# A mirrored table copied by another DMA queue, a mirrored column by matrix products, mirrored rows in four transfers

## The chip, the cores and the metric

The kernel runs on one core of one Trainium2 chip. The metric is the device time of one execution in microseconds (us). Profiles come from the hardware profiler, of one execution. Engines: PE is TensorE (PEld its weight loads), ACT ScalarE, DVE VectorE, POOL GpSimd, SP SyncE. Here SP issues nearly all DMAs, and POOL the few that copy from DRAM to DRAM with rows turned round; each of the two has a DMA queue of its own.

## The reference

Two independent layers over 2048 tokens of width 448, their outputs side by side:

```python
# A: Fourier mixing, real part of a 2-D DFT
a = einsum("bsd,ed->bse", x, dft_hid_re);  b = einsum("bsd,ed->bse", x, dft_hid_im)
y = einsum("ts,bse->bte", dft_seq_re, a) - einsum("ts,bse->bte", dft_seq_im, b)
# B: attention with 16 heads of 28
q, k, v = split(x @ wqkv);  p = softmax(q @ k.T * 28 ** -0.5);  o = (p @ v) @ wo
out = concatenate([y, o], axis=-1)
```

The inputs are float32, and so is the output.

## The kernel before

**Work.** Attention (B) runs head by head: scores (L1404, 128 keys by 512 queries), exp on ACT (L1408), and a pack of 32 products with the values (L1415) for every 16 scores. Scores need ACT, which is slower than PE at this, so PE fills the time between them with the other work, in this order: the projections to q, k and v (L619), the feature transform of layer A (L871, `hidden_both`), its sequence transform, real part (part 0) and imaginary part (part 1) (L1145, `sequence_halved`), and the output projection (L1646).

**Symmetry in layer A.** The DFT tables are symmetric, so the kernel multiplies with a quarter of the sequence table and reads the rest of it only to compare it with the mirrored quarter: the differences go through small products too, and a flag at the end repeats everything in a plain way (`If(again != 0)`) if a difference is above 2^-17 of the largest entry. For the comparison three things are needed in mirrored order:

- the mirrored table `turned_d` (basd in the profile): for each part 8 x 128 rows of 2 KB, read from the table with a negative row step and written to DRAM, in 9 DMAs of up to 256 KB (`turn_table`). The sequence transform loads it (L1118).
- the mirrored column: the column 0 of block row 8, 4 x 128 numbers in reverse order. `turn_table` copies it from the table to DRAM (`row_d`, rowd in the profile), with a last dimension of one element; `columns` loads it (`turn`, L1019) and subtracts it from the column itself (L1026).
- the mirrored rows of the transformed features (`turned_ab`, abt in the profile): for each of four groups one DMA of 4 x 127 rows of 1792 bytes, from `ab_d` (abd in the profile), plus a small one for the first row (`turn_rows`, L940 and L944). `combine` loads them (L957).

All three kinds of copies are issued by POOL, through `move`.

**Order.** The program's order is written out ahead of time by a planner (`Schedule.run`) in the kernel's Python code: each task has engines with assumed durations, a key (its due time in the planner's units), dependencies and slots of buffers. Each engine takes the ready task with the lowest key; a task with `hold=True` isn't taken before the work on PE has come near its key. A DMA task on SP is modelled with a size (the KB moved), an extra latency, a flow of all DMAs and at most 8 in flight; a task of `move` only with a duration on POOL and a latency, without any flow. Each engine then runs its own list in order, and a wait in it holds all that stands behind.

```python
    def dma(key, emit, size=256, extra=0.0, n=1, **kw):
        return sch.add({"SP": 0.4}, key, lambda e: emit(), dmas=[(size, extra)] * n, **kw)
    def move(key, emit, d, lat, **kw):
        return sch.add({"POOL": d}, key, lambda e: emit(), lat=lat, **kw)
    ...
    for part in range(2):
        turn_table(part, 120.0 + 200.0 * part)
    turn_rows()
```

The feature transform starts at the key `h_at` (304.8 by the planner's constants) and ends at `s_at` (474.1). Buffers that matter here: `kept`, 20 tiles of 128 x 2 x 512 floats, which hold exp's output, the loads and results of layer A and staged outputs; 8 PSUM banks.

**Start.** SP loads the inputs (xb, wqkv, xa), stores the first q and k to DRAM (L664, L665, qkd in the profile) and loads pieces of them (L1385, qb), with which PE computes a first maximum (L1388). The values' projection (L619, "wd,xt") runs around these.

Of the kernel before, what the change touches and what calls it, by code (L numbers as in the profile page):

```python
# [11 lines left out]
F32 = mybir.dt.float32  # L12
# [316 lines left out]
def tile_kernel(ctx, tc, xa, wre, wim, wd, xb, wqkv, wo, out):  # L329
# [25 lines left out]
    row_d = [dram.tile([FT, P], F32, name=f"rowd{i}") for i in range(2)]  # L355
# [4 lines left out]
    ident = new("ident", [P, P])  # L360
# [26 lines left out]
    turn = new("turn", [P, FT])  # L387
# [26 lines left out]
    make_identity(nc, ident)  # L414
    nc.gpsimd.memset(sums, 0.0)
# [434 lines left out]

    def hidden_both(ready):
        for g in PAIRS_AT:
            x, ld = rows_both(g, fkey(0, 0) - 13)
            for a in range(2):
                st = g + a * HT
                key = fkey(1, F_ROWS)
                hi, lo, h, l = folded(x, ld, a, key - 9)
                pair = kept_s.slot()
                of = lambda w, i: w.t[:ROWS[i % 2], i]
                seq = []  # L860
                for i in range(4):
                    c0, c1 = (0, EVEN) if i < 2 else (EVEN, 2 * MAIN)
                    seq += [(hi, i, lambda i=i: table(i, "main"), 0, 2 * MAIN, M448), (lo, i, lambda i=i: table(i, "hi"), c0, c1, MLOW),
                            (hi, i, lambda i=i: low_at(i), c0, c1, MLOW)]
                rest = [(hi, i, lambda i=i: table(i, "rest"), 0, 2 * REST, M448) for i in range(4)]
                at = key
                ends = []
                for b, (seq, o) in enumerate(((seq, fill_s.slot()), (rest, fill_s.slot()))):
                    for n, (w, i, y, c0, c1, d) in enumerate(seq):
                        def emit(e, w=w, i=i, y=y, c0=c0, c1=c1, o=o, n=n, m=len(seq) - 1):  # L870
                            nc.tensor.matmul(o.t[:, c0:c1], of(w, i), y(), start=n == 0, stop=n == m)  # L871
                        last[0] = pe(at, emit, d=d, deps=[last[0], *([h, *ready] if n == 0 else [l] if n == 1 else [])],
                                     use=[hi, lo, o, *low_in, *([pair] if n == len(seq) - 1 else [])])
                        at += d
                    ways = ((0, 0, EVEN), (1, EVEN, 2 * MAIN)) if b == 0 else ((None, 0, 2 * REST),)
                    for e, c0, c1 in ways:
                        to = lambda pair=pair, e=e: pair.t[:, :, MAIN:D] if e is None else pair.t[:, :, e:MAIN:2]
                        ends.append(sch.add({"ACT": 0.43 if e is None else 0.3, "DVE": 0.53 if e is None else 0.32}, key - 10,
                                            lambda w, o=o, to=to, c0=c0, c1=c1: copy_of(w, to(), halves(o.t[:, c0:c1])), deps=[last[0]], use=[o, pair]))
                ab_done[st] = dma(key - 10, lambda pair=pair, st=st: nc.sync.dma_start(ab_d[st % HT][st // HT].rearrange("b p d -> p b d"), pair.t[:, :, :D]), 448, deps=ends, use=[pair])  # L880
# [26 lines left out]
    def move(key, emit, d, lat, **kw):  # L907

        return sch.add({"POOL": d}, key, lambda e: emit(), lat=lat, **kw)

    base_turned, ab_turned, row_turned = {}, {}, {}

    def turn_table(part, key):
        src = wim if part else wre
        row, to = NT * P, turned_d[part]
        for n, p in enumerate(range(1, P, 16)):
            r = min(16, P - p)

            def put(p=p, r=r):
                nc.gpsimd.dma_start(rows_at(to, p * FT * P, [[P * FT * P, HT], [FT * P, r], [1, FT * P]]),  # L920
                                    rows_at(src, (P - p) * row, [[P * row, HT], [-row, r], [1, FT * P]]))
            base_turned[part, n] = move(key + n * 4, put, 1.5, 12.0, hold=True)

        def first():
            nc.gpsimd.dma_start(rows_at(to, 0, [[P * FT * P, HT], [1, FT * P]]), rows_at(src, P, [[P * row, HT], [1, FT * P]]))
            at = HT * P * row
            nc.gpsimd.dma_start(rows_at(row_d[part], 1, [[P, FT], [1, P - 1], [1, 1]]), rows_at(src, at + (P - 1) * row, [[P, FT], [-row, P - 1], [1, 1]]))
            nc.gpsimd.dma_start(rows_at(row_d[part], 0, [[P, FT], [1, 1]]), rows_at(src, at + P, [[P, FT], [1, 1]]))
        row_turned[part] = base_turned[part, HT] = move(key + HT * 4, first, 2.5, 12.0, hold=True)

    def turn_rows():
        none = kept_s.slot()
        z = pool(0.0, lambda: nc.gpsimd.memset(none.t[:1], 0.0), 0.6, use=[none])
        ab_turned[0, 0] = dma(0.0, lambda: nc.sync.dma_start(rows_at(turned_ab[0], 0, [[P * D, 2], [1, D]]), none.t[:1, :, :D]), 4, deps=[z], use=[none])
        ab_turned[0, 1] = dma(0.0, lambda: nc.sync.dma_start(rows_at(turned_ab[0], 2 * P * D, [[P * D, 2], [1, D]]), none.t[:1, :, :D]), 4, deps=[z], use=[none])
        for g in range(FT):
            far = HT - 1 - g

            def put(g=g, far=far):
                nc.gpsimd.dma_start(rows_at(turned_ab[g], D, [[P * D, 4], [D, P - 1], [1, D]]), rows_at(ab_d[far], (P - 1) * D, [[P * D, 4], [-D, P - 1], [1, D]]))  # L940
            ab_turned[g, 2] = move(0.0, put, 1.5, 16.0, deps=[ab_done[far], ab_done[far + HT]])
            if g:
                def first(g=g):
                    nc.gpsimd.dma_start(rows_at(turned_ab[g], 0, [[P * D, 4], [1, D]]), rows_at(ab_d[HT - g], 0, [[P * D, 4], [1, D]]))  # L944
                ab_turned[g, 0] = move(0.0, first, 1.2, 5.0, deps=[ab_done[HT - g], ab_done[NT - g]])

    def combine(part, at, after):
        half = lambda s, i, n=D: s.t[:, i, :n]
        minus, plus = (ALU.add, ALU.subtract) if part else (ALU.subtract, ALU.add)

        def group(g):
            key = at(g)
            x, y, m = kept_s.slot(), kept_s.slot(), kept_s.slot()
            ld = dma(key, hold=True, emit=lambda: nc.sync.dma_start(x.t[:, :, :D], ab_d[g][:, part].rearrange("a p d -> p a d")),
                     size=448, deps=[ab_done[g], ab_done[g + HT]], use=[x])

            lm = dma(key + 1, hold=True, emit=lambda: nc.sync.dma_start(m.t[:, :, :D], turned_ab[g][:, part].rearrange("a p d -> p a d")),  # L957
                     size=448, deps=[ab_turned[g, n] for n in range(3) if (g, n) in ab_turned], use=[m])
# [16 lines left out]
        def plain(h):  # L975
            key = at(h) + 1
            x = kept_s.slot()
            ld = dma(key, hold=True, emit=lambda: nc.sync.dma_start(x.t[:, :, :LOW], ab_d[FT + h][:, part, :, :LOW].rearrange("a p d -> p a d")),
                     size=226, deps=[ab_done[FT + h], ab_done[FT + h + HT]], use=[x])
# [32 lines left out]
    def columns(part, key, after, after_all):  # L1012
# [6 lines left out]
        lr = dma(key, lambda: nc.sync.dma_start(turn, row_d[part].rearrange("f p -> p f")), 16, extra=4.0, deps=[*after, row_turned[part]])  # L1019
        if part:  # L1020
            lr = pool(key, lambda: nc.gpsimd.memset(turn[:1, FT - 1:], 0.0), 0.1, deps=[lr])
# [3 lines left out]
        for t in (FT, HT + FT):  # L1025
            d.append(dve(key, lambda t=t: nc.vector.tensor_tensor(dmid[:, t:t + FT], raw[:, t:t + FT], back(turn, 0, FT), op=op), 0.2, deps=[ld, lr]))  # L1026
# [5 lines left out]
    def special(part, key, after):  # L1032
# [5 lines left out]
        def put():  # L1038
            nc.sync.dma_start(w.t.rearrange("p a b -> p (a b)")[:65:32], rows_at(src, FT * P, [[0, 3], [P * row, HT], [1, P]]))
            nc.sync.dma_start(x.t[:65:32, :, :D], rows_at(ab_d[FT], part * P * D, [[0, 3], [2 * P * D, 2], [1, D]]))  # L1040
            if part == 0:
                nc.sync.dma_start(x.t[:65:32, 0, D:D + 1], rows_at(src, HT * P * row + FT * P, [[0, 3], [1, 1]]))
# [5 lines left out]
        if part == 0:  # L1048
            one = lambda p0=0: x.t[p0:96, 0, D:D + 1]
# [3 lines left out]
        both = lambda i, p0=0, p1=96: x.t[p0:p1, i, :D]  # L1053
# [471 lines left out]
    for part in range(2):  # L1525
        turn_table(part, 120.0 + 200.0 * part)
# [251 lines left out]
```

## Time and profile before

| | |
|---|---|
| time, median of 3 runs | 842.19 us (836.09 to 845.36) |
| the profiled execution | 837.84 us, span 836.0 us |
| mean granted TensorE clock | 0.975 |
| PE busy | 804.3 us (96%) |
| ACT busy | 572.4 us (68%) |
| DVE busy | 441.5 us (53%) |
| POOL busy | 73.6 us (9%) |
| moved by DMA | 155.29 MB, mean 186 GB/s |

The profiled execution is one of the program's; its span runs from the first to the last instruction. "Granted clock" is the share of the full TensorE clock that was let through; a PE that is busy at a low clock does less. A row of the chain of work gives its start, its duration and what it was. Rows of an engine's timeline give start, duration, line, operation, tiles (written <- read) and how often; in brackets the idle time before it and what ended that. For DMAs issued by POOL the last number is the median time from issue to landing.

### The profile page before, as it was taken

How to read it: one execution, taken by the hardware profiler on the slowest of the kernel's cores; microseconds unless marked ns; L12 is line 12 of the kernel's file. 1: busy time of each engine (PE TensorE's matmuls, PEld its weight loads, DVE VectorE, ACT ScalarE, POOL GpSimd, SP SyncE). 2: the span in 40 equal slices, each digit the busy share in tenths (PEclk: the TensorE clock that was granted, in tenths of full speed). 3: DMA queues.
4: the chain of work that ended last, by engine and by line, in shares of the span. 5: the costliest groups of instructions: out<-in, count | busy, mean ns of one | idle time of the engine just before them, and what ended most of it. 6: DMA issues, size and time to landing. Idle time of an engine off the chain costs nothing.

```text
span 836.0 us, 14227 instructions
## 1 busy us (share of the span) xinstructions
PE 804.3 (96%) x4713; PEld 483.5 (58%) x4713; DVE 441.5 (53%) x913; ACT 572.4 (68%) x1162; POOL 73.6 (9%) x230
## 2 busy tenths in 40 slices
PE   8779999999999889999999999999999999999986
PEld 6667555575565455566554555555545555555666
DVE  6523224354153223253432877868898876794551
ACT  5202887657878646887878676777787777878922
POOL 5200000000010200000000111011111110110000
PEclk9889999999999969999999999999999999999999
DMA  7996856643354764545546887686878677764533
GB/s 246 229 193 208 267 161 204 197 165 104 118 165 111 148 107 116 169 133 183 146 130 201 208 255 239 199 264 191 261 162 276 212 217 250 236 219 147 164 124 107
DMA packets 149159, 155.29 MB, mean 186 GB/s; under 512 B 41992, under 2 KB 118374, under 8 KB 149078
## 3 DMA queue, kind: packets, MB, share of 16 engines
q1 hardware_dynamic: 143638, 146.40, 60.6%
q0 software_dynamic: 5440, 7.91, 3.2%
q8 instruction: 39, 0.64, 0.3%
q14 instruction: 42, 0.34, 0.2%
HBM read 112.78 MB, written 50.99 MB: 196 GB/s over the span
## 4 chain that ended last, share of the span: by engine, by line
PE 81%; DMA 14%; ACT 1%; DVE 1%; SPq 1%; issue 1%; DVEq 0%; ACTq 0%
PE bank L1404 30%; PE bank L1415 25%; PE bank L1145 9%; PE bank L619 8%; PE bank L871 4%; DMA qkd<-kept 2%; DMA abd<-kept 2%; PE bank L1646 2%; DMA kept<-xb 2%; DMA rd<-sm 1%; DMA wraw<-wqkv 1%; DMA kept<-abd 1%; DMA kept<-rd 1%; DMA kept<-ond 1%; DMA qb<-qkd 1%; DMA fard<-kept 1%
## 5 line engine op out<-in xcount | busy, mean ns | idle before, releaser
L1408 ACT ACTIVATE kept<-bank 128x512 f32<-128x512 f32 x1024 | 510.3, 672 | 155.0 <-PE bank L1404 148.2
L1404 PE MATMUL bank<-q,k 85*128 85x512 f32 x1024 | 369.6, 430 | 5.1 <-ACT kept L1408 4.4
L1404 PEld LDWEIGHTS bank<-q,k 85*128 85x128 f32 x1024 | 186.0, 191 | 108.7 <-issue 42.2
L1415 PE MATMUL bank<-kept,v 128*32 128x512 f32 x2048 | 235.0, 599 | 0.0
L1415 PEld LDWEIGHTS bank<-kept,v 128*32 128x32 f32 x2048 | 61.0, 110 | 131.8 <-issue 126.5
L1102 DVE TENSOR_REDUCE diff<-zt 128x1 f32<-128x512 bf16 x112 | 76.7, 685 | 7.7 <-DVE zt L1188 0.5
L1145 PE MATMUL bank<-zt 128*128 128x226 bf16 x448 | 77.5, 267 | 0.0
L470 DVE COPY kept<-bank 128x226 f32<-128x226 f32 (+3 forms) x59 | 28.3, 502 | 88.9 <-PE bank L871 65.7
L619 PE MATMUL bank<-xt,whi 128*128 128x512 f32 x196 | 69.0, 398 | 2.6 <-DVE xt L464 1.9
L1145 PEld LDWEIGHTS <-zt 128*128 128x128 bf16 x448 | 31.1, 100 | 33.8 <-issue 23.1
L871 PE MATMUL bank<-wd,whi 128*128 128x450 f32 (+3 forms) x128 | 45.2, 399 | 4.1 <-DVE kept L470 4.1
L619 PE MATMUL bank<-xt,wlo 128*128 128x512 f32 x112 | 44.1, 395 | 0.0
L619 PEld LDWEIGHTS bank<-xt,whi 128*128 128x128 f32 x196 | 36.4, 189 | 13.1 <-DVE xt L464 2.6
L619 PE MATMUL bank<-wd,xt 128*128 128x448 f32 x176 | 41.5, 393 | 0.0
L1145 PE MATMUL bank<-xt,whi 128*128 128x448 f32 (+1 forms) x128 | 40.1, 334 | 0.0
L619 PEld LDWEIGHTS bank<-wd,xt 128*128 128x128 f32 x176 | 35.6, 206 | 5.1 <-issue 1.3
L1391 DVE STREAM_TRANSPOSE kept<-bank 128x512 f32<-128x512 f32 (+1 forms) x20 | 14.3, 713 | 39.1 <-PE bank L1388 39.1
L1468 ACT ACTIVATE kept<-bank 128x512 f32<-128x512 f32 (+1 forms) x19 | 11.3, 593 | 33.6 <-PE bank L1415 32.0
L1188 DVE TENSOR_TENSOR zt<-wdraw,xraw 128x508 bf16<-128x508 f32 x28 | 19.1, 682 | 28.6 <-PE bank L1145 26.3
L871 PEld LDWEIGHTS bank<-wd,whi 128*128 128x128 f32 (+1 forms) x128 | 24.9, 204 | 9.4 <-DVE kept L470 4.5
L470 DVE CAST wd<-bank 128x512 fp32r<-128x512 f32 x9 | 6.2, 692 | 42.3 <-PE bank L619 42.3
L1145 PEld LDWEIGHTS bank<-xt,whi 128*128 128x128 f32 x128 | 24.5, 197 | 4.4 <-ACT kept L1408 2.2
(172 smaller groups left out, 699.2 us busy)
## 6 DMA issues: line engine op xcount, KB each, us to landing
wdraw<-wim SPq DMA_DIRECT2D x38, 256.0 KB
qkd<-wd SPq DMA_DIRECT2D x32, 256.0 KB
wdraw<-wre SPq DMA_DIRECT2D x32, 256.0 KB
q<-qkd SPq DMA_DIRECT2D x64, 112.0 KB
k<-qkd SPq DMA_DIRECT2D x64, 112.0 KB
abd<-kept SPq DMA_DIRECT2D x16, 448.0 KB
qkd<-kept SPq DMA_DIRECT2D x24, 256.0 KB
xraw<-wre SPq DMA_DIRECT2D x24, 256.0 KB
```

Source lines behind the costliest of these rows:

```text
L470: nc.vector.tensor_copy(dst, src)
L619: nc.tensor.matmul(o.t[:, :cols], w(), x(), start=(i == 0), stop=(i == n - 1))
L871: nc.tensor.matmul(o.t[:, c0:c1], of(w, i), y(), start=n == 0, stop=n == m)
L1102: seen.append(dve(key, lambda: nc.vector.tensor_reduce(dst, src(), axis=AX.X, op=ALU.max, apply_absolute_value=True), 0.68, deps=deps, use ...
L1145: nc.tensor.matmul(o.t[:, at0:at0 + n], cut_of(w.t, e, c), x(), start=first, stop=stop)
L1188: e.tensor_tensor(turned(dl.t, 1, 1, P - 1), mirror(r.t), read(base.t, 1, 1, P - 1), op=minus)
L1391: r = dve(key, lambda o=o, mt=mt: nc.vector.transpose(mt.t[:32 * n, 0], o.t[:32 * n]), 0.64, deps=[m], acq=[mt], use=[o], own=RAW_S)
L1404: m = pe(key, lambda e: nc.tensor.matmul(b.t, KT[h][kt // 4].t[:KR + 1, kt % 4 * P:(kt % 4 + 1) * P], q.t[:KR + 1, :], start=True, stop=True),
L1408: return act(key - 20, lambda: nc.scalar.activation(p.t, b.t, AF.Exp, scale=SCALE), deps=[m], use=[b, pair])
L1415: nc.tensor.matmul(o.t[j * VW:(j + 1) * VW, :], VT[h].t[:, kt // 4, kt % 4, :], tiles[i // 2].t[:, i % 2, :], start=(kt < 4 // len(cs)), s ...
L1468: a = act(key - 20, lambda: nc.scalar.activation(osb.t[:n * VW], o.t[:n * VW], AF.Copy, accum_out=sums[:n * VW, g:g + 1]), deps=[dep], use ...
L1646: nc.tensor.matmul(o.t[:, :D], a(), b(), start=(i == 0), stop=(i == 8 and n < N_HELD))
```

## The change

1. The mirrored table is copied by SP's queue instead of POOL's, as tasks of `dma` with their size, and at other keys: part 0 from `h_at - 30` in steps of 8, part 1 from `h_at + 50` in steps of 10, nine copies each.
2. The mirrored column is no longer copied. `columns` turns it with two products on PE: the loaded column times a reversed identity (a DVE copy of the identity with a reversed read), plus the first row's elements times a row of the identity; the subtractions read the result from PSUM. `row_d` and `turn` are gone.
3. The mirrored rows of a group go in four DMAs of 32 (the last 31) rows by 4, still on POOL. The row of zeros for the first group is written later, after the first features are stored.
4. The tiles that carry features (`pair`, `x`, `m`) hold their two rows of 448 floats one behind the other (`tight`) instead of at 512 floats' distance, and the loads of `plain` fetch all 448 columns instead of 226.

```diff
-    ident = new("ident", [P, P])
+    wide_ident = new("ident", [P, P + 1])
+    ident = wide_ident[:, :P]
...
+    def tight(t):
+        return t.rearrange("p a b -> p (a b)")[:, :2 * D].rearrange("p (a b) -> p a b", a=2)
...
-    def turn_table(part, key):
+    def turn_table(part, key, step):
         src = wim if part else wre
         row, to = NT * P, turned_d[part]
-        for n, p in enumerate(range(1, P, 16)):
-            r = min(16, P - p)
+        for n in range(HT + 1):
+            p = 16 * n - 15 if n else 0
+            r = min(16, P - p) if n else 1
 
             def put(p=p, r=r):
-                nc.gpsimd.dma_start(rows_at(to, p * FT * P, [[P * FT * P, HT], [FT * P, r], [1, FT * P]]),
-                                    rows_at(src, (P - p) * row, [[P * row, HT], [-row, r], [1, FT * P]]))
-            base_turned[part, n] = move(key + n * 4, put, 1.5, 12.0, hold=True)
-        def first():
...
-        row_turned[part] = base_turned[part, HT] = move(key + HT * 4, first, 2.5, 12.0, hold=True)
+                nc.sync.dma_start(rows_at(to, p * FT * P, [[P * FT * P, HT], [FT * P, r], [1, FT * P]]),
+                                  rows_at(src, (P - p) * row if p else P, [[P * row, HT], [-row, r], [1, FT * P]]))
+            base_turned[part, n] = dma(key + n * step, put, 256 if n else 16, extra=4.0, hold=True)
...
-            def put(g=g, far=far):
-                nc.gpsimd.dma_start(rows_at(turned_ab[g], D, [[P * D, 4], [D, P - 1], [1, D]]), rows_at(ab_d[far], (P - 1) * D, [[P * D, 4], [-D, P - 1], [1, D]]))
-            ab_turned[g, 2] = move(0.0, put, 1.5, 16.0, deps=[ab_done[far], ab_done[far + HT]])
+            def put(n, g=g, far=far):
+                p, r = 32 * n + 1, 32 - n // 3
+                nc.gpsimd.dma_start(rows_at(turned_ab[g], p * D, [[P * D, 4], [D, r], [1, D]]),
+                                    rows_at(ab_d[far], (P - p) * D, [[P * D, 4], [-D, r], [1, D]]))
+            ab_turned[g, 2] = [pool(0.0, lambda n=n, put=put: put(n), 1.2, lat=8.0, deps=[ab_done[far], ab_done[far + HT]]) for n in range(4)]
...
-        lr = dma(key, lambda: nc.sync.dma_start(turn, row_d[part].rearrange("f p -> p f")), 16, extra=4.0, deps=[*after, row_turned[part]])
+        o, flip = bank_s.slot(), kept_s.slot()
+        n = FT - part
+        f = dve(key - 5, lambda: nc.vector.tensor_copy(flip.t[:, 0, :P], at_of(ident, P, [[-1, P]])), 0.25, use=[flip], deps=after)
+
+        def turned_column(e):
+            nc.tensor.matmul(o.t[:, :FT], flip.t[:, 0, :P], raw[:, :FT], start=True, stop=False)
+            nc.tensor.matmul(o.t[:, :n], ident[:1], raw[:1, 1:n + 1], start=False, stop=True)
+        lr = pe(key, turned_column, d=0.5, deps=[ld, f], use=[o, flip], mode=1)
...
-    for part in range(2):
-        turn_table(part, 120.0 + 200.0 * part)
+    turn_table(0, h_at - 30, 8)
+    turn_table(1, h_at + 50, 10)
     turn_rows()
```

More of the change, by code (lines that the diff above doesn't have):

```diff
@@ L386, in tile_kernel @@
     edge = new("edge", [P, 4, NT])
-    turn = new("turn", [P, FT])
     dmid = new("dmid", [P, NT])
@@ L934, in turn_rows @@
-        ab_turned[0, 0] = dma(0.0, lambda: nc.sync.dma_start(rows_at(turned_ab[0], 0, [[P * D, 2], [1, D]]), none.t[:1, :, :D]), 4, deps=[z], use=[none])
-        ab_turned[0, 1] = dma(0.0, lambda: nc.sync.dma_start(rows_at(turned_ab[0], 2 * P * D, [[P * D, 2], [1, D]]), none.t[:1, :, :D]), 4, deps=[z], use=[none])
+        z = pool(0.0, lambda: nc.gpsimd.memset(none.t[:1], 0.0), 0.6, deps=[ab_done[PAIRS_AT[0]]], use=[none])
+        ab_turned[0, 0] = [dma(0.0, lambda a=a: nc.sync.dma_start(
+            rows_at(turned_ab[0], 2 * a * P * D, [[P * D, 2], [1, D]]), tight(none.t)[:1]), 4, deps=[z], use=[none]) for a in range(2)]
@@ L944, in first, with of_rows @@
                     nc.gpsimd.dma_start(rows_at(turned_ab[g], 0, [[P * D, 4], [1, D]]), rows_at(ab_d[HT - g], 0, [[P * D, 4], [1, D]]))
-                ab_turned[g, 0] = move(0.0, first, 1.2, 5.0, deps=[ab_done[HT - g], ab_done[NT - g]])
+                ab_turned[g, 0] = [pool(0.0, first, 1.2, lat=8.0, deps=[ab_done[HT - g], ab_done[NT - g]])]
+    def of_rows(t, part):
+        return t[:, part].rearrange("a p d -> p a d")
     def combine(part, at, after):
-        half = lambda s, i, n=D: s.t[:, i, :n]
+        half = lambda s, i, n=D: tight(s.t)[:, i, :n]
         minus, plus = (ALU.add, ALU.subtract) if part else (ALU.subtract, ALU.add)
@@ L953, in group @@
             x, y, m = kept_s.slot(), kept_s.slot(), kept_s.slot()
-            ld = dma(key, hold=True, emit=lambda: nc.sync.dma_start(x.t[:, :, :D], ab_d[g][:, part].rearrange("a p d -> p a d")),
+            ld = dma(key, hold=True, emit=lambda: nc.sync.dma_start(tight(x.t), of_rows(ab_d[g], part)),
                      size=448, deps=[ab_done[g], ab_done[g + HT]], use=[x])
-            lm = dma(key + 1, hold=True, emit=lambda: nc.sync.dma_start(m.t[:, :, :D], turned_ab[g][:, part].rearrange("a p d -> p a d")),
-                     size=448, deps=[ab_turned[g, n] for n in range(3) if (g, n) in ab_turned], use=[m])
+            lm = dma(key + 1, hold=True, emit=lambda: nc.sync.dma_start(tight(m.t), of_rows(turned_ab[g], part)),
+                     size=448, deps=[d for n in (0, 2) for d in ab_turned[g, n]], use=[m])
             zs = []
@@ L977, in plain @@
             x = kept_s.slot()
-            ld = dma(key, hold=True, emit=lambda: nc.sync.dma_start(x.t[:, :, :LOW], ab_d[FT + h][:, part, :, :LOW].rearrange("a p d -> p a d")),
-                     size=226, deps=[ab_done[FT + h], ab_done[FT + h + HT]], use=[x])
+            ld = dma(key, hold=True, emit=lambda: nc.sync.dma_start(tight(x.t), of_rows(ab_d[FT + h], part)),
+                     size=448, deps=[ab_done[FT + h], ab_done[FT + h + HT]], use=[x])
             for j in range(2):
@@ L1025, in columns @@
         for t in (FT, HT + FT):
-            d.append(dve(key, lambda t=t: nc.vector.tensor_tensor(dmid[:, t:t + FT], raw[:, t:t + FT], back(turn, 0, FT), op=op), 0.2, deps=[ld, lr]))
+            d.append(dve(key, lambda t=t: nc.vector.tensor_tensor(dmid[:, t:t + FT], raw[:, t:t + FT], back(o.t, 0, FT), op=op), 0.2, deps=[ld, lr], use=[o]))
         seen.append(dve(key, lambda: nc.vector.tensor_reduce(
@@ L1039, in put @@
             nc.sync.dma_start(w.t.rearrange("p a b -> p (a b)")[:65:32], rows_at(src, FT * P, [[0, 3], [P * row, HT], [1, P]]))
-            nc.sync.dma_start(x.t[:65:32, :, :D], rows_at(ab_d[FT], part * P * D, [[0, 3], [2 * P * D, 2], [1, D]]))
+            nc.sync.dma_start(tight(x.t)[:65:32], rows_at(ab_d[FT], part * P * D, [[0, 3], [2 * P * D, 2], [1, D]]))
             if part == 0:
-                nc.sync.dma_start(x.t[:65:32, 0, D:D + 1], rows_at(src, HT * P * row + FT * P, [[0, 3], [1, 1]]))
+                nc.sync.dma_start(x.t[:65:32, 1, CH - 1:], rows_at(src, HT * P * row + FT * P, [[0, 3], [1, 1]]))
         ld = dma(key, put, 12, n=3 - part, extra=1.0, deps=[*zs, ab_done[FT], ab_done[HT + FT], *after], use=[w, x])
@@ L1052, in special @@
                             deps=[a], use=[x]))
-        both = lambda i, p0=0, p1=96: x.t[p0:p1, i, :D]
+        both = lambda i, p0=0, p1=96: tight(x.t)[p0:p1, i]
         u = dve(key, lambda: nc.vector.tensor_tensor(both(0), both(0), both(1), op=ALU.subtract if part else ALU.add), 0.6, deps=[ld], use=[x])
```

24 lines of the change are left out of this document (8 added, 16 removed).

## The prediction

> **What bounds the kernel now.** I read the page first, then a table of stages, then the chain that ended last, and last the issues of POOL, SP and TensorE around the two holes that this showed.
>
> ```profile
> span 836.0 us, 14227 instructions
> PE 804.3 (96%) x4713; PEld 483.5 (58%) x4713; DVE 441.5 (53%) x913; ACT 572.4 (68%) x1162; POOL 73.6 (9%) x230
> ```
>
> TensorE (PE) is busy for 96% of the span, so little seems to be left. But a busy PE may run at half its clock. The stage table gives, after the stage and its length, busy time and number of instructions of PE, PEld, DVE, ACT and POOL, then the granted clock, the DMA share and GB/s.
>
> ```profile
> 33.60:38.20 4.60, 0.01 (x1) 0.01 (x1) 1.46 (x6) 0.00 (x0) 0.00 (x0) 0.85 1.56 117
> 38.20:52.60 14.40, 14.37 (x57) 12.49 (x57) 4.66 (x13) 0.00 (x0) 0.00 (x0) 0.81 1.01 82
> 52.60:57.20 4.60, 0.05 (x1) 0.00 (x0) 0.37 (x2) 0.00 (x0) 0.00 (x0) 1.00 0.93 321
> 57.20:65.30 8.10, 7.62 (x28) 6.07 (x28) 2.97 (x7) 0.00 (x0) 0.00 (x0) 0.79 0.72 206
> 65.30:285.00 219.70, 219.26 (x1235) 134.15 (x1235) 77.04 (x153) 157.97 (x322) 10.19 (x15) 1.00 0.56 174
> 285.00:320.00 35.00, 26.78 (x123) 17.29 (x127) 11.46 (x25) 17.10 (x33) 0.55 (x2) 0.71 0.71 101
> 320.00:425.00 105.00, 105.00 (x654) 62.87 (x647) 40.56 (x95) 84.89 (x174) 4.51 (x5) 1.00 0.49 153
> ```
>
> PE has two holes, 33.6 to 65.3 and 285 to 320 us, each with idle time and a low clock after it. Around them PE is full at clock 1.00. In both the DMA engines are busy yet move little: share 1.01 at 82 GB/s against 0.56 at 174. The chain names DMAs there, and POOL's issues and their landing times (last column) name the cause.
>
> ```profile
> 33.83 19.66 DMA qkd<-kept
> 53.56 3.61 DMA qb<-qkd
> 60.98 3.88 DMA qb<-qkd
> 292.50 16.09 DMA abd<-kept
> ...
> 18.40 3.15 POOL L920 DMA_DIRECT2D basd<-wre  x5 [2.40 <-issue]
> 31.47 1.16 POOL L927 DMA_DIRECT2D rowd<-wre  x1
> 237.49 1.80 POOL L920 DMA_DIRECT2D basd<-wim  x3
> 269.83 1.12 POOL L940 DMA_DIRECT2D abt<-abd  x1 [30.54 <-DMA abd<-kept]
> 283.86 1.15 POOL L927 DMA_DIRECT2D rowd<-wim  x1 [8.84 <-DMA abt<-abd]
> ...
> abt<-abd POOLq DMA_DIRECT2D x4, 889.0 KB, 14.0
> basd<-wim POOLq DMA_DIRECT2D x7, 256.0 KB, 12.4
> rowd<-wre POOLq DMA_DIRECT2D x1, 2.0 KB, 20.0
> rowd<-wim POOLq DMA_DIRECT2D x1, 2.0 KB, 21.4
> ```
>
> The transfer rowd moves 2 KB, the mirrored column, one 4-byte element at a time. It is in flight from 31.5 to 51.5 and from 283.9 to 305.3, and this is where the holes lie. SP's stores issued in those times (qkd at 33.83, abd at 292.50) land after 19.66 and 16.09 us. So the two holes are the price of two 2 KB gathers, with the bulk copies ahead of them as helpers.
>
> **The change part by part.** *The mirrored column by two products* removes both gathers (and the two loads of turn).
>
> First hole. PE's issues there, and SP's:
>
> ```profile
> 28.79 4.82 PE L619 MATMUL bank<-wd,xt 128*128 128x448 f32 x23
> 38.23 0.65 PE L1388 MATMUL bank<-qb,kb 56*64 56x512 f32 x1 [4.62 <-DMA qb<-qkd]
> 38.81 13.84 PE L619 MATMUL bank<-wd,xt 128*128 128x448 f32 x56
> 57.22 0.61 PE L1388 MATMUL bank<-qb,kb 56*64 56x512 f32 x1 [4.57 <-DMA qb<-qkd]
> 57.76 6.68 PE L619 MATMUL bank<-wd,xt 128*128 128x448 f32 x25
> ...
> 18.54 4.73 SPq L589 DMA_DIRECT2D wraw<-wqkv  x3
> 31.61 0.83 SPq L1385 DMA_DIRECT2D qb<-qkd  x1
> 33.83 6.00 SPq L664 DMA_DIRECT2D qkd<-kept  x1
> 45.89 0.42 SPq L665 DMA_DIRECT2D qkd<-kept  x1
> ```
>
> 23 products in 4.82 us, the last of them some 0.4 us long, is 0.20 us each at full clock. Hence 23 + 56 + 25 = 104 products need 20.9 us, and three of L1388 at about 0.24 another 0.7: 21.6 us from 28.79. The third L1388 begins when its qb lands, 60.98 + 3.88 = 64.86. The hole costs at most 64.9 − 28.8 − 21.6 = 14.5 us.
>
> What is late next? PE would reach its first L1388 at 33.6. Its qb, issued at 31.61, lands 3.6 us later if it lands like the one of 53.56: 35.2, a wait of 1.6 us. That goes too if SP gets there earlier: three loads at 18.54 took 4.73 us to issue, against 1.26 at the 0.42 of an unhindered issue, while the table's copies ran on POOL's queue, and these are moved away. PE's second L1388 would come at 33.6 + 0.24 + 56 × 0.20 = 45.0. The six stores from 33.83 on then take 2.5 us instead of 12.5 (to 46.3); with 5 us to land (estimated, above the 3.9 of the rows) and a qb of 3.6, its data is there at 44.9. The third qb follows 7.4 us of SP issues after the second (53.56 to 60.98), landing at 41.3 + 7.4 + 3.9 = 52.6, while PE comes at 45.0 + 0.24 + 5.0 = 50.3: 2.3 us of wait, or none with SP ahead by 3.5. So between 10.6 (both waits stay) and 14.5 us; I take **12.5**.
>
> Second hole. The packs of L1415 come once for every 16 scores and mark the pace:
>
> ```profile
> 281.28 3.64 PE L1415 MATMUL bank<-kept,v 128*32 128x512 f32 x32
> 317.20 3.57 PE bank L1415 x32
> 327.86 3.57 PE bank L1415 x32
> 367.91 3.57 PE bank L1415 x32
> ```
>
> From 327.86 to 367.91 there are four steps of 10.0 us. From 281.28 to 317.20 there are two, in 35.9 us: 15.9 lost, of which some 0.9 comes back because the fill work got ahead meanwhile (my estimate). At least 11 go with the gather (PE idles 8.2 us of 285 to 320, and about 3 of the time at half clock follow from that). I take **14**: abt, which stays, ran again at about 329 and 371, in a stage where PE has 105.00 of 105.00 us.
>
> *The products*: four f32 products of four columns, a DVE copy with a reversed read, one bank for a few us.
>
> ```profile
> L1495 PE MATMUL bank<-kept,fold x8: 592/605/617, 762.4 to 798.0; 128*32 128x512 f32 x8
> ```
>
> An f32 product of 512 columns occupies 0.6 us; four columns cost less. Four of them are between 0 and 2.4 us, and I take 1.0 in all with the turns between kinds of work. The copy lies on DVE (53% busy).
>
> *The table on SyncE's queue*: 18 copies, keyed from 30 before the transform to 130 after its start in the planner's units. The transform takes 169 of these units.
>
> ```profile
> L871 PE MATMUL bank<-wd,whi x128: 360/370/743, 238.8 to 434.4; 128*128 128x450 f32 x32, 96*128 96x450 f32 x32, 128*128 128x446 f32 x32, 96*128 96x446 f32 x32
> L1118 SPq DMA_DIRECT2D xraw<-basd x14: 366/408/790, 450.0 to 693.9; - x14
> L1253 SPq DMA_DIRECT2D out<-fard x9: 694/731/809, 676.2 to 789.8; - x9
> 240.00:245.00 5.00, 5.00 (x41) 2.02 (x40) 3.04 (x7) 2.20 (x5) 0.00 (x0) 1.00 0.87 287
> ```
>
> At 195.6 us for 169 units the last copy of the first table goes out near 278 and of the second near 389, before the first read at 450.0: nobody waits for them. They have no waits of their own, so SP is held for 18 × 0.73 us (L1253 is a DRAM to DRAM copy of the same queue) over some 170 us. What is queued behind them are the loads of q, k, xa and the stores of abd. In 240 to 245, with three copies in flight and everything else, the engines were busy 0.87 × 5 = 4.4 us, so a copy takes at most 1.5 us. A load behind one is late by that, and PE stays hidden while loads are issued further ahead than that. From 0 (hidden; PE was full at 240 to 245) to 18 × 1.5 = 27 us (every one on the path); nearest to the row at 240 I take **1.5**.
>
> The Trainium skill (DMA: Bandwidth & Descriptors, "Why a DMA increments its semaphore by 16 and not by 1") says that a DMA runs on the largest number of engines up to 16 that divides the outermost size of both sides, and that SP's always take the lowest-numbered ones. By that rule a copy, outermost size 8, loads only the same half of the engines, twice as long, and everything else of SP waits in that half; by the row the copies cost the 1.5 us above, by the rule, an estimate, twice that. The row of 240 cannot show which engines were busy.
>
> *Mirrored rows in four transfers*: the same 889 KB for a group, POOL issuing four times (1.12 us each at most, POOL is 9% busy). Of the chain's rows above none is a transfer of abt, so neither gain nor loss on the path: 0, between −1 (its landing of 14.0 us shortens and small transfers beside it are quicker) and +1. The tight tiles move the same rows (plain loads twice the bytes, eight times): 0.
>
> Sum: 837.84 (the profiled execution) − 12.5 − 14 + 1 + 1.5 = 813.8 us. The median of the three runs, 842.19, stands 4.4 above that execution. The same change against the median gives 818.2; as I cannot tell whether the spread comes from the holes, I put the forecast between, at **817**.
>
> **Rivals.** *One hole stays.* For it: at 271 to 284 small transfers were already slow, with abt and the copies in flight and no rowd yet; at the start all loads come at once. Against: the stage table is full at 329 and 371 beside abt alone. It gives 842.2 − 12.5 = about 829.
>
> *Neither goes*, because bulk traffic makes the holes and the gathers only coincide with them: about 840. Against: GB/s falls to 82 instead of rising, in both.
>
> *The copies clog SP's queue* (the other side). They now stand in the same queue as the loads that PE needs. Landing of basd<-wim was 12.4 us on POOL's queue. The point from which this decides is 25.5 / 18 = 1.4 us lost for each copy. At 2 us each it gives 842 − 26.5 + 1 + 36 = about 853. Against it: L1253 copies 224 KB pieces on SP without a hole.
> The Trainium skill (the same page, "Queues, rings and completion order") says that an engine takes turns between queues packet by packet, but serves one queue in order: by this a load beside POOL's copy shares with it, and behind SP's own copy it waits for all of it. No run so far shows it for a table copy on SP.
>
> *It doesn't do what it says*: the column made by products differs in its last bits, the flag at the end is set and all work is repeated, well over 1600 us.
>
> **How the numbers follow.** Both holes go: 0.68, 806 to 826. One stays: 0.13, 824 to 833. Neither: 0.08, 834 to 846. Copies clog: 0.09, from 838 up. Repeated: 0.02. The lowest, 806, is 837.8 less 14.5 and 15.9, and about the other costs at nothing; the upper end of the range, 830, takes in the case of one hole, which together leaves out 2 in 10. Faster by over 1% (below 833.8, about what this measurement can tell): 0.81; within 1%: 0.09; slower: 0.10.
>
> **What would show it.** Right: no qkd store landing after 19 us, no idle PE before L1388 at 33 to 57, clock 1.00 in 285 to 320, packs of L1415 every 10 us throughout, 18 basd issues on SP between about 220 and 390. Wrong: new PE waits for q, k or xa loads within a few us of a basd issue; ACT waiting for abd stores as before; PE waiting at the new column's products for its load or its reversed copy. The planner orders everything anew from changed tasks, so small waits elsewhere, of either sign, would make it wrong by a few us.

## The result, and the profile after

| | before | after |
|---|---|---|
| time, median of 4 runs each, side by side | 843.78 us (836.09 to 847.43) | 816.64 us (814.54 to 817.81) |
| ratio, 95% interval | | 0.9687 (0.9615 to 0.976) |
| the profiled execution | 837.84 us | 814.54 us |
| mean granted TensorE clock | 0.975 | 0.989 |

The change makes the kernel 3.1% faster (2.4 to 3.9%), 27.1 us between the medians and 23.3 between the two profiled executions. The forecast was 817 us. Here and below a ratio leaves out executions that took over 1.5% longer than the fastest of the same kernel in the same job, while medians and ranges count all of them. In the kernel after, line numbers are shifted by 3 to 4 in the attention part: scores are L1408, the packs of products with the values L1419, the first maximum L1392. The table's copies are L921, the two new products L1023 and L1024.

The page of the kernel after, its span and busy times:

```profile
span 812.7 us, 14203 instructions
PE 798.2 (98%) x4721; PEld 477.1 (59%) x4721; DVE 442.1 (54%) x920; ACT 570.1 (70%) x1157; POOL 63.5 (8%) x220
```

PE's busy time fell by 6 us though it does a little more work: it spends less of it at half clock (mean granted clock 0.989 instead of 0.975). Five rows of the prediction's table of stages, for the kernel after:

```profile
33.60:38.20 4.60, 4.60 (x25) 4.25 (x24) 1.62 (x6) 0.00 (x0) 0.00 (x0) 1.00 0.41 134
38.20:52.60 14.40, 14.40 (x69) 12.36 (x68) 7.02 (x18) 0.60 (x1) 0.00 (x0) 1.00 0.44 130
52.60:57.20 4.60, 4.60 (x22) 3.50 (x21) 2.17 (x5) 0.60 (x1) 0.00 (x0) 1.00 0.83 235
285.00:320.00 35.00, 35.00 (x209) 18.53 (x211) 12.15 (x29) 28.89 (x60) 3.42 (x5) 1.00 0.54 162
320.00:425.00 105.00, 104.26 (x612) 60.53 (x608) 36.34 (x88) 82.33 (x170) 6.30 (x9) 0.95 0.52 160
```

Both holes are filled: PE is busy for the whole of each stretch up to 320 us, at clock 1.00. But the last row, which was 105.00 at 1.00 before, is now 104.26 at 0.95. Something was lost there.

How much at each place? There are 2048 products with the values in each kernel. The lines of these products in both (number, shortest/median/longest in ns, first and last start), before and then after:

```profile
L1415 PE MATMUL bank<-kept,v x2048: 589/592/1062, 89.9 to 795.6; 128*32 128x512 f32 x187
...
L1419 PE MATMUL bank<-kept,v x2048: 592/592/1062, 75.1 to 772.7; 128*32 128x512 f32 x187
```

The first comes 14.8 us earlier, the last 22.9. Between them, the chain's rows of the packs after:

```profile
287.47 3.57 PE bank L1419 x32
...
337.95 3.57 PE bank L1419 x32
```

They are the same packs as the rows at 317.20 and 367.91 of before (the 20th and the 25th of 64): a lead of 29.7 and 30.0 us. So the gain is 14.8 at the start and 15 at the second hole, together 30, and **7 us of it are given back after 400 us**. Here is where. First the stages, then the chain at this place, last VectorE's wait, all of the kernel after:

```profile
395.00:405.00 10.00, 9.26 (x55) 4.45 (x53) 2.68 (x6) 7.66 (x18) 1.84 (x3) 1.00 0.50 159
405.00:415.00 10.00, 10.00 (x37) 6.25 (x40) 3.31 (x8) 6.75 (x14) 0.00 (x0) 0.52 0.50 142
465.00:470.00 5.00, 3.00 (x21) 1.61 (x24) 4.90 (x14) 2.83 (x6) 0.00 (x0) 1.00 0.76 238
...
397.95 4.39 DMA kept<-abd
402.36 0.63 DVE kept L1058
403.02 0.58 ACT xt L1059
403.60 0.49 ACT kept L1412
404.13 1.52 PE bank L1408 x3
...
DVE kept L1058 <- DMA kept<-abd: 5.3, 1, 5.3
```

The sequence transform's special rows are loaded from abd (`special`, L1044 and L1058). VectorE waits 5.3 us for the load, ScalarE's exp stands behind the split that VectorE delays, and PE stands for 0.74 us. That alone is little. But then follow 10 us at clock 0.52, in which PE does about half of what it could: 37 matmuls, where before did 64 in the same 10 us of its own span at full clock (first row below). At a clock of 0.52, 10 us lose 4.8 (an estimate). A second stand of 2.0 us comes at 466. The sum, 0.7 + 4.8 + 2.0 and the new products' 1.2, is 8.7 us; before had a stand of 0.7 nearby too, and no low clock behind it:

```profile
405.00:415.00 10.00, 10.00 (x64) 5.90 (x62) 7.30 (x18) 8.42 (x18) 0.53 (x1) 1.00 0.45 135
425.00:430.00 5.00, 4.26 (x25) 2.11 (x28) 1.59 (x5) 5.00 (x12) 0.00 (x0) 1.00 0.41 136
430.00:435.00 5.00, 5.00 (x38) 2.28 (x30) 2.00 (x6) 3.00 (x8) 0.00 (x0) 1.00 0.32 30
```

The starts of the packs check this sum. The packs that begin at 429.04 and 439.01 us before begin at 397.96 and 412.33 after, so the lead falls there from 31.1 to 26.7 us. Before then loses 1.3 us itself, at 465 to 470, where its clock is 0.69 although no idle time of PE is listed (busy 5.00 of 5.00). At the pack behind the second stand the lead is 24.7 (493.36 against 468.69), and at the last pack 23.0. So about 5 of the 7 us go at the two places shown, and the rest later.

### The profile page after: what moved, and what is told of

The parts are those of the page before. It is cut to its first block, busy times and chain, and to the rows that moved or that the text cites. A ratio compares the mean times of both kernels' runs of the same rounds, so it can differ in the third digit from the quotient of the medians.

```text
span 812.7 us, 14203 instructions
## 1 busy us (share of the span) xinstructions
PE 798.2 (98%) x4721; PEld 477.1 (59%) x4721; DVE 442.1 (54%) x920; ACT 570.1 (70%) x1157; POOL 63.5 (8%) x220
## 4 chain that ended last, share of the span: by engine, by line
PE 86%; DMA 6%; ACT 3%; SPq 2%; DVE 1%; issue 1%; POOL 0%; ACTq 0%; DVEq 0%
PE bank L1408 30%; PE bank L1419 26%; PE bank L619 12%; PE bank L1149 8%; PE bank L874 5%; PE bank L1650 3%; ACT kept L1412 2%; DMA xraw<-wre 2%; PE bank L1681 1%; DMA wraw<-wre 1%; PE bank L1392 1%; DMA kept<-xb 1%; DMA wdraw<-wim 1%; SPq L1130 1%; DMA kept<-abd 1%
## 5 line engine op out<-in xcount | busy, mean ns | idle before, releaser
L1408 PE MATMUL bank<-q,k 85*128 85x512 f32 x1024 | 368.4, 428 | 0.8 <-ACT kept L1412 0.7
L1408 PEld LDWEIGHTS bank<-q,k 85*128 85x128 f32 x1024 | 184.7, 190 | 104.9 <-issue 38.6
L1419 PE MATMUL bank<-kept,v 128*32 128x512 f32 x2048 | 236.2, 602 | 0.4 <-ACT kept L1412 0.4
L1419 PEld LDWEIGHTS bank<-kept,v 128*32 128x32 f32 x2048 | 60.4, 110 | 134.1 <-issue 127.9
L470 DVE COPY kept<-bank 128x224 f32<-128x224 f32 (+3 forms) x61 | 29.4, 502 | 109.9 <-PE bank L874 88.1
L619 PE MATMUL bank<-wd,xt 128*128 128x448 f32 x176 | 37.4, 368 | 0.0
L619 PEld LDWEIGHTS bank<-wd,xt 128*128 128x128 f32 x176 | 32.7, 188 | 3.7 <-issue 1.0
L1149 PEld LDWEIGHTS bank<-xt,whi 128*128 128x128 f32 x128 | 24.7, 198 | 5.7 <-DVE kept L1233 2.3
L874 PEld LDWEIGHTS bank<-wd,whi 128*128 128x128 f32 (+1 forms) x128 | 23.7, 193 | 6.0 <-ACT kept L1412 3.6
L468 ACT ACTIVATE kept<-bank 128x512 fp32r<-128x512 f32 (+4 forms) x20 | 11.5, 591 | 20.1 <-PE bank L619 7.5
```

Source lines behind the costliest of these rows:

```text
L468: nc.scalar.activation(dst, src, AF.Copy)
L470: nc.vector.tensor_copy(dst, src)
L619: nc.tensor.matmul(o.t[:, :cols], w(), x(), start=(i == 0), stop=(i == n - 1))
L1149: nc.tensor.matmul(o.t[:, at0:at0 + n], cut_of(w.t, e, c), x(), start=first, stop=stop)
L1408: m = pe(key, lambda e: nc.tensor.matmul(b.t, KT[h][kt // 4].t[:KR + 1, kt % 4 * P:(kt % 4 + 1) * P], q.t[:KR + 1, :], start=True, stop=True),
L1419: nc.tensor.matmul(o.t[j * VW:(j + 1) * VW, :], VT[h].t[:, kt // 4, kt % 4, :], tiles[i // 2].t[:, i % 2, :], start=(kt < 4 // len(cs)), s ...
```

## The experiments

The theory: the two element-wise copies of the mirrored column (rowd) make both holes, in that other stores beside them do not land. Rivals: POOL's bulk copies of the table make them; the size of the mirrored rows' transfers; and, for the last 7 us, the table's copies in SP's queue. Kernels run together share their runs of the kernel before, and only such ones are compared closely.

**Each part alone.** First job, before there 834.9 us. `col_only` is the kernel before with the column by products, and nothing else:

```diff
-            nc.gpsimd.dma_start(rows_at(row_d[part], 1, [[P, FT], [1, P - 1], [1, 1]]), ...)
-            nc.gpsimd.dma_start(rows_at(row_d[part], 0, [[P, FT], [1, 1]]), ...)
...
+            nc.tensor.matmul(o.t[:, :FT], flip.t[:, 0, :P], raw[:, :FT], start=True, stop=False)
+            nc.tensor.matmul(o.t[:, :n], ident[:1], raw[:1, 1:n + 1], start=False, stop=True)
```

> The kernel before with the mirrored column alone made by two products: the element-wise copy of the column to DRAM is gone, the table's and the rows' copies stay on POOL's queue at their old keys. Theory (the element copies make both holes): both holes close, 15 us at the start and 14 in the transform, about 815 to 822 us; the part that comes from the table's copies on POOL stays below 3 us. Rival (bulk copies make the holes, the element copies only coincide): the holes stay for the most part, 835 to 843 us.

Measured 821.21 us (818.78 to 821.49), ratio 0.9825 (0.9735 to 0.9914): 13.7 us faster between the medians (0.9 to 2.7% by the ratio), and 6.0 behind the whole change (as `rows_whole` below). Two short stands are left, at places where the table's copies run on POOL's queue. The stages of `col_only`:

```profile
30.00:35.00 5.00, 2.90 (x14) 2.08 (x13) 4.07 (x11) 1.77 (x4) 0.00 (x0) 1.00 0.98 309
272.00:278.00 6.00, 4.24 (x26) 2.31 (x19) 2.03 (x4) 4.06 (x9) 0.00 (x0) 1.00 0.37 118
```

At 30 to 35 the engines move 309 GB/s at share 0.98: I read that stand as a queue of real traffic, not as the old hole. At 272 the chain names a store of SP (rd, the sums of the softmax) that was issued at 259.96, beside five of the table's copies, and landed after 11.16 us. So bulk copies hold up a store too, but PE's two stands come to 2.1 and 1.8 us.

`table_only` is the kernel before with the table on SP's queue; the element copies (`turn_column`) stay on POOL:

```diff
-        turn_table(part, 120.0 + 200.0 * part)
+    turn_table(0, h_at - 30, 8)
+    turn_table(1, h_at + 50, 10)
+        turn_column(part, 152.0 + 200.0 * part)
```

> The kernel before with the table alone copied by SP's queue during the transform; the element-wise copy of the column stays on POOL at its old keys, the rows stay in one transfer a group. Theory: both element copies still hold up the stores issued in their 20 us, so 833 to 843 us, less only if they now fall where nobody waits. Rival (bulk copies): 815 to 822 us.

Measured 833.49 us (826.74 to 834.7), ratio 0.9984 (0.9946 to 1.0023): no difference. The landing times of the element copies, and PE at the first hole (its timeline, in brackets the idle time before):

```profile
rowd<-wre POOLq DMA_DIRECT2D x1, 2.0 KB, 16.5
rowd<-wim POOLq DMA_DIRECT2D x1, 2.0 KB, 23.7
...
48.38 0.68 PE L1391 MATMUL bank<-qb,kb 56*64 56x512 f32 x1 [4.26 <-DMA qb<-qkd]
```

No copy of the table is on POOL's queue here, and the holes are there: at the first one a store of q and k issued at 28.73 us lands after 16.08, with nothing but the element copies on POOL's queue. They need no help. (At the second hole, mirrored rows went out on POOL just ahead of the element copy.) The table's move is worth 1.4 us (not told from nothing) while the holes stand. Once they are gone, 6.0 us separate `col_only` from `rows_whole`, but these hold the later zero rows and the tight tiles besides the table's move, and no run has one of the three alone there.

`rows_whole` is the kernel after with each group's mirrored rows in one transfer again:

```diff
-            ab_turned[g, 2] = [pool(0.0, lambda n=n, put=put: put(n), 1.2, lat=8.0, ...) for n in range(4)]
+            ab_turned[g, 2] = [pool(0.0, put, 1.5, lat=16.0, ...)]
```

> The changed kernel with the mirrored rows of a group again in one transfer of 4 x 127 rows. Theory: no transfer of these rows was on the path, so within 2 us of the changed kernel's 816.6; each lands after about 14 us instead of 6. Rival (the split gave a part of the gain, since one large transfer keeps few DMA engines busy for long): 820 to 826 us, with PE idle beside one of the four transfers.

Measured 815.23 us (814.22 to 816.16), ratio 0.976 (0.9672 to 0.9847). Landing times, of after and then of `rows_whole`, and two stages of the latter:

```profile
abt<-abd POOLq DMA_DIRECT2D x12, 224.0 KB, 5.8
...
abt<-abd POOLq DMA_DIRECT2D x4, 889.0 KB, 14.3
...
285.00:295.00 10.00, 9.67 (x46) 5.87 (x50) 5.58 (x13) 4.72 (x9) 0.00 (x0) 0.66 0.48 135
405.00:415.00 10.00, 10.00 (x69) 5.69 (x61) 3.84 (x9) 8.22 (x17) 0.00 (x0) 1.00 0.41 132
```

The transfer lands 8.5 us later and the kernel is no slower. Yet the order is another one: a stretch at low clock has come at 286 and the one at 405 has gone, in the one profile of each. Equal times can hide two changes.

`copies_twice` is the kernel after with every copy of the table issued a second time, to a place that nobody reads:

```diff
+                for t in (to, more_d[part]):
+                    nc.sync.dma_start(rows_at(t, ...), ...)
-            base_turned[part, n] = dma(key + n * step, put, 256 if n else 16, extra=4.0, hold=True)
+            base_turned[part, n] = dma(key + n * step, put, 256 if n else 16, extra=4.0, n=2, hold=True)
```

> The changed kernel with each of the 18 table copies on SP's queue issued a second time into a spare tensor, both known to the planner: 36 copies instead of 18. Theory (a copy costs PE 0.1 us or less): 816 to 820 us. Rival (copies in SP's queue cost as the forecast's bound says, 1.5 us each): 840 us or more. If the lead lost between 400 and 510 us is owed to copies, it doubles to some 10 us: 821 to 823.

Measured 817.5 us (812.55 to 823.11), ratio 0.9812 (0.9709 to 0.9916). Against `rows_whole` of the same job that is 2.3 us for 18 more copies, 0.13 each, and at the far ends of the two ranges 8.9 us, 0.5 each. The rival of a clogged queue needed 1.4.

**The cause alone.** Second job, before there 836.71 us; the kernel after, `after_again`, ran in it as the mark:

> The changed kernel itself, once more, as the one to which the next three are compared on the same chip: 814 to 818 us.

814.76 us (812.11 to 817.56), ratio 0.9728 (0.9685 to 0.9771). `gather_back` is the kernel after with the 508-element copy of the column put back, on POOL at its old key; nobody reads it:

```diff
+            nc.gpsimd.dma_start(rows_at(row_d[part], 1, [[P, FT], [1, P - 1], [1, 1]]),
+                                rows_at(src, at + (P - 1) * row, [[P, FT], [-row, P - 1], [1, 1]]))
+        sch.add({"POOL": 1.7}, key, lambda e: put(), lat=12.0, hold=True)
```

> The changed kernel with nothing but the two element-wise copies of the column to DRAM added again on POOL's queue (508 elements each, at the old keys; nobody reads the result). Theory (the element copies hold up all stores issued meanwhile): both holes come back beside these copies, in part, since no bulk copies run beside them now: 826 to 836 us. Rival (they hurt only because kernel and planner waited for their result, or only together with bulk copies): 815 to 820 us.

Measured 830.21 us (824.5 to 834.39), ratio 0.9891 (0.9843 to 0.994): 15.5 us for two 2 KB copies without a reader. Of `gather_back`: their landing times, POOL's issue of the second, the store on the chain beside it, and PE's stages there.

```profile
rowd<-wre POOLq DMA_DIRECT2D x1, 2.0 KB, 14.7
rowd<-wim POOLq DMA_DIRECT2D x1, 2.0 KB, 17.4
...
264.68 1.16 POOL L931 DMA_DIRECT2D rowd<-wim  x1
...
264.06 17.26 DMA rd<-sm
...
275.00:280.00 5.00, 5.00 (x36) 2.93 (x25) 0.00 (x0) 2.88 (x7) 0.00 (x0) 1.00 0.00 0
280.00:285.00 5.00, 1.86 (x10) 1.21 (x8) 0.00 (x0) 3.26 (x7) 0.00 (x0) 0.89 0.10 16
285.00:290.00 5.00, 0.60 (x2) 0.52 (x3) 1.82 (x4) 0.00 (x0) 0.00 (x0) 0.50 0.46 141
```

A store of SP (rd) that went out 0.6 us before the copy lands about when it does, 17.26 us later, and all that stands behind it runs dry. In 275 to 280 the DMA engines show share **0.00** and 0 GB/s: the records show nothing moving, and still neither transfer is complete.

`gather_apart` is the same with the elements written 512 bytes apart:

```diff
-    row_d = [dram.tile([FT, P], F32, ...
+    row_d = [dram.tile([FT, P, P], F32, ...
-            nc.gpsimd.dma_start(rows_at(row_d[part], 1, [[P, FT], [1, P - 1], [1, 1]]),
+            nc.gpsimd.dma_start(rows_at(row_d[part], P, [[P * P, FT], [P, P - 1], [1, 1]]),
```

> As the one before, but the 508 elements of each copy are written 512 bytes apart, not side by side into 2 KB. Same reads, same number of 4-byte writes. If the cause is that all the small writes meet in the same few lines of memory, the copy lands in under 8 us and the time is within 3 us of the changed kernel's. If each 4-byte write to DRAM costs, it lands after 16 to 24 us as before and the time is that of the kernel with the copies side by side. If the number of elements read with a stride costs, also the latter.

Measured 817.48 us (816.06 to 820.29), ratio 0.9766 (0.9726 to 0.9805). Landing times, and the stage that stood still above:

```profile
rowd<-wre POOLq DMA_DIRECT2D x1, 2.0 KB, 6.7
rowd<-wim POOLq DMA_DIRECT2D x1, 2.0 KB, 8.0
...
275.00:280.00 5.00, 5.00 (x36) 2.89 (x38) 4.33 (x11) 5.00 (x11) 0.00 (x0) 1.00 0.69 220
```

The reads are the same, as many and as scattered, mirrored rows go out on POOL just ahead of the copy as before, and 12.7 of the 15.5 us are gone. It is the 4-byte **writes side by side in the same 2 KB of DRAM** that hold up the others, not the gather. The Trainium skill (DMA: Bandwidth & Descriptors, "Specifications") says that a transfer below 512 bytes is done by reading, changing and writing back. The trace bears out that such elements are slow (2 KB land after 6.7 us here, 224 KB of mirrored rows in the same run after 5.8), but the rule speaks of size alone, and by size both kernels are alike: 14.7 and 17.4 us against 6.7 and 8.0 show that their neighbourhood counts, which the rule does not say. Distances other than side by side and 512 bytes were not tried.

**The remedy without the change.** Third job, before there 837.84 us. `col_apart` is the kernel *before* in all else; only the elements of row_d are 512 bytes apart (both copies, and the load that reads them):

```diff
-            nc.gpsimd.dma_start(rows_at(row_d[part], 1, [[P, FT], [1, P - 1], [1, 1]]), ...)
-            nc.gpsimd.dma_start(rows_at(row_d[part], 0, [[P, FT], [1, 1]]), ...)
+            nc.gpsimd.dma_start(rows_at(row_d[part], P, [[P * P, FT], [P, P - 1], [1, 1]]), ...)
+            nc.gpsimd.dma_start(rows_at(row_d[part], 0, [[P * P, FT], [1, 1]]), ...)
...
-    nc.sync.dma_start(turn, row_d[part].rearrange("f p -> p f"))
+    nc.sync.dma_start(turn, row_d[part][:, :, 0].rearrange("f p -> p f"))
```

> The kernel before with one thing changed: the column's elements are written to DRAM 512 bytes apart instead of side by side, and loaded from there. No products, the table's copies stay on POOL. Theory (small writes side by side are the cause): both holes close as with the products, 816 to 824 us. Rival (the copies' other work, reading one element of each 8 KB row, or their number, matters with bulk copies beside them): 830 to 840 us.

Measured 817.8 us (807.83 to 825.6, 4 runs), ratio 0.9773 (0.9647 to 0.9899). Three changed address patterns are worth 20 us between the medians and some 19 by the ratio, with a wide spread (8 to 30 by its interval). Landing times, and what stays of the first hole:

```profile
rowd<-wre POOLq DMA_DIRECT2D x1, 2.0 KB, 6.3
rowd<-wim POOLq DMA_DIRECT2D x1, 2.0 KB, 4.6
...
35.00:40.00 5.00, 2.61 (x6) 2.00 (x7) 1.69 (x4) 0.00 (x0) 0.00 (x0) 0.56 1.04 346
```

Here the engines move 346 GB/s: I read this remainder as the table's bulk copies at the start, as in `col_only`.

**The 7 us after 400.** `special_later`, in the second job, is the kernel after with one number of the planner changed, the latency that it assumes for the special rows' loads:

```diff
-        ld = dma(key, put, 12, n=3 - part, extra=1.0, deps=[*zs, ...
+        ld = dma(key, put, 12, n=3 - part, extra=6.0, deps=[*zs, ...
```

> The changed kernel with one number of the planner changed: the small loads of the special rows (12 KB) get 6 us more latency than 1 us more. In the changed kernel's trace DVE stood still for 5.3 us for such a load at 398, ACT and PE behind it, and PE's clock was halved for 10.2 us after a gap of 0.7 us. Theory (that wait starts the half clock): the half clock at 405 goes, 4 to 6 us less than the changed kernel, 809 to 813 us. Rival (the gap has another source, or the next late load takes its place): 814 to 818 us.

Measured 811.7 us (809.65 to 813.99), ratio 0.9698 (0.9659 to 0.9737), against 814.76 of the kernel after in the same job. VectorE's wait for the special rows is gone there, and the stage reads:

```profile
405.00:415.00 10.00, 9.39 (x60) 5.68 (x61) 4.79 (x11) 8.52 (x20) 0.00 (x0) 1.00 0.61 198
```

The third job ran it again in five rounds (`special_late5`), beside `special_edge`, which has the first column's edge loads go out during the feature transform as well:

```diff
-        edge_ready[part] = [dma(key + 20 + i, ..., deps=after_all) for i in range(1, 4)]
+        edge_ready[part] = [dma(key + 20 + i if part else key - 110 + 20 * i, ..., hold=not part) ...]
...
-    columns(0, s_at - 14, [h_last], [h_last])
+    columns(0, s_at - 14, [h_last], [])
```

> The changed kernel with the later special rows once more, in more rounds, as the one the next is compared with: 810 to 814 us.

> The same, and the three loads of the edge columns of part 0 (2048 elements of 4 bytes each, to SBUF) planned during the feature transform instead of at the start of the sequence transform, where DMA moved 34 to 99 GB/s beside them. Theory (they delay the loads around them): PE's gap of 1 to 3 us near 466 to 476 goes, 808 to 811 us. Rival (reads of 4 bytes into SBUF cost nothing that PE sees): no difference, 810 to 814 us.

811.23 us (808.33 to 814.85), ratio 0.9754 (0.9693 to 0.9815), and 811.79 us (807.8 to 814.95), ratio 0.9752 (0.9688 to 0.9817). The edge loads change nothing that shows; the stand near 466 to 476 that they were to remove is in neither of the two profiles (PE is busy for 30.00 of 30.00 us from 455 to 485 in both). `special_late5` has the lowest median of this study, though its lead over the kernel after, 3.1 us in the one job that has both, is of the size of either's spread. And its profile corrects the reading of the first one:

```profile
405.00:415.00 10.00, 8.74 (x43) 5.36 (x45) 5.21 (x12) 7.04 (x15) 0.00 (x0) 0.66 0.49 147
465.00:470.00 5.00, 5.00 (x39) 2.00 (x38) 4.76 (x11) 2.05 (x5) 0.00 (x0) 1.00 1.03 329
```

A stand near 405 is there in both executions, and the low clock in this one only. The stands are not the old one: PE waits 0.83 us for a load of q in the first and 1.26 us for a copy of VectorE in the second. Whether the low clock follows near 405 is then not settled by the special rows' loads; what both executions lack is the stand at 466 (the first has one of 1.2 us at 475 to 480).

The mark's own profile (`after_again`) shows that both places are the kernel's and no chance of one execution: a stand of 1.6 us before 405.27, clock 0.54 from 405 to 415, and 2.7 us of idle PE in 465 to 470. Its lead, measured by the same packs, falls from 30.8 to 25.8 us at the first place and is 21.8 at the end. In `special_later` it falls from 31.4 to 30.5 and is 30.7 at the end; in `special_late5` it falls from 30.6 to 26.9 and is still 29.8 at the end. So the 7 us are gone in both, though the first place still costs 3.7 of them in the second.

## Why the prediction was right, and where its terms were off

Median 816.64 against 817; the profiled execution 814.54 against a sum of 813.8. The mechanism was right, but that the sum is closer than its terms is luck: two misses cancel, 3.2 us more gained at the holes than put down and some 4 more lost behind them.

**First hole, 14.8 instead of 12.5, beyond the bound of 14.5.** PE's timeline of the kernel after:

```profile
31.38 0.44 PE L1392 MATMUL bank<-qb,kb 56*64 56x512 f32 x1
...
43.29 0.44 PE L1392 MATMUL bank<-qb,kb 56*64 56x512 f32 x1
...
48.93 0.45 PE L1392 MATMUL bank<-qb,kb 56*64 56x512 f32 x1
```

The first maxima stand at 31.4, 43.3 and 48.9 where 33.6, 45.0 and 50.3 to 52.6 were worked out. They show no idle time before them, so the choice between the bounds should have fallen on the upper one. (The lower bound was too low besides: a third load that lands at 52.6 delays PE by 2.3 us in all, whether or not PE has waited 1.6 before, so the bound is 12.2 and not 10.6.) And the whole row is some 2 us early, which the working did not have: PE was ready for the first maximum at 33.6 before and is at 31.4 after. From there to the third maximum 13.7 us are saved, within the bounds; 1.2 are lost again up to the first pack. SP's issues show one thing that happens ahead of it, before and after:

```profile
9.52 0.75 SPq L934 DMA_DIRECT2D abt<-kept  x1
...
11.39 5.83 SPq L556 DMA_DIRECT2D kept<-xb  x9
...
5.43 8.99 SPq L556 DMA_DIRECT2D kept<-xb  x12
```

The stores of the zero rows (abt) stood among the input loads; the change writes them later, and nine loads move up. This line of the change was given no term, on the queue that fills PE at the start. But it is not the whole of the 2.2 us: `col_only` and `table_only` still have these stores among the loads, and PE is ready for its first maximum at 32.2 and 32.1 there, against 31.1 to 31.7 in all the kernels with the later stores. So 0.4 to 1.1 us are theirs at most, and where the rest comes from stays open. The step that failed is that the working starts at 28.79 us and puts nothing for what comes ahead of it.

**Second hole, 14.9 instead of 14** (29.7 at 317.20 less 14.8): right within 1 us.

**Products, 1.2 instead of 1.0.** PE's timeline at part 0 (the left out line is the second product), 0.62 us from the first of them to the next score, and 0.63 at part 1:

```profile
437.24 0.39 PE L1023 MATMUL bank<-edge,kept 128*128 128x4 f32 x2
...
437.86 1.43 PE L1408 MATMUL bank<-q,k 85*128 85x512 f32 x5
```

**Copies on SP, 1.5 of a range from 0 to 27.** Two readings bear out the low end. SP's issues after (shortest/median/longest in ns, first and last start):

```profile
L921 SPq DMA_DIRECT2D basd<-wre x9: 648/701/949, 194.9 to 267.8; - x9
L921 SPq DMA_DIRECT2D basd<-wim x9: 673/692/702, 274.6 to 376.5; - x9
```

The last ones come at 268 and 377 (278 and 389 were expected), 0.70 us each (0.73), while PE is busy at clock 1.00 from 285 to 320; and 18 more of them cost 2.3 us. The rule that the prediction set against this, from the Trainium skill (DMA: Bandwidth & Descriptors, "Why a DMA increments its semaphore by 16 and not by 1"), would have every copy on one half of the engines. No run here shows which engines were used, and the doubled price that was worked out from it, 3 us for 18 copies, cannot be told from the 2.3 measured.

**Split rows, 0**: right in sum (815.23 against 814.76 to 816.64), by way of two changes that cancel, as far as one profile of each can tell.

**What was missing: the 7 us after 400**, where +2.5 stood in the sum for all added work. The prediction named this itself as what it could not see, small waits of a new order, but sized it at "a few us". A wait of 0.74 us of PE and the low clock behind it come to 5.5 by the estimate above, and to 4.4 by the packs; that the wait brings the low clock is not shown.

**The reading of the cause was half right.** The element copies are the cause: `gather_back` brings 15.5 us back. But two phrases fail. The bulk copies are no helpers of it (`table_only` has none of the table on that queue, and its copies land after 16.5 and 23.7 us); they cost something of their own, 2.1 and 1.8 us of idle PE at the two places in `col_only`. And "busy yet move little" was read as work: with the other traffic thin, share is 0.00 during the same wait.

The rivals (one hole stays, neither goes, the clogged queue, the repeated work): none came. What stays open is where the adjacent writes are held, in the memory or in the DMA engines' write side, and why the clock falls after some short stands.

## What to carry to other kernels

Look in the list of transfers for the small ones with a long landing time: a copy to DRAM of single elements into neighbouring places holds back the stores of other queues too, and the loss shows as waits for those. Write such elements far apart (here 512 bytes), or make the turned column on an engine: in the kernel before the first was worth some 19 us (8 to 30), the second alone 13.7 between the medians. When a large stall goes, compare the lead of the two kernels at paired instructions along the whole span, since a good sum can hide a stall removed and one acquired.

## What the runs showed that was not expected

A copy of 508 elements, 2 KB in all, delays a store on another queue by about as long as it takes itself (17.26 beside 17.4 us), with the DMA engines at share 0.00 for 5 us of it. Mirrored rows had gone out on its queue just ahead; with the same ahead of it and the elements 512 bytes apart, the engines move 220 GB/s in the same stage.

A stand of PE well under a microsecond may be followed by a long stretch at half clock, or by none: 0.74 us and then 10 us at 0.52 in the kernel after; 0.74 us and then clock 1.00 in the kernel before at 425 to 435. And the clock can be low with no stand listed at all: 0.69 in the kernel before at 465 to 470, with PE busy for 5.00 of 5.00 us. The Trainium skill (TensorE: Matmul & The Clock Gate, "HAM oscillation — how this bites in real kernels") puts the rule at no idle gaps above about 3.4 us. This case does not bear that out as a safe limit: the gap before the 10 us was a fifth of it.
